# Two pads in SBUF and a new timetable for the operand sums of an expert stage on TensorE

## The chip, the core and the metric

One core of a Trainium2 chip runs the whole program in one launch. The metric is the device time of the launch in microseconds (us), taken as the median of several runs. Beside the timed runs there is one execution with a hardware profile; its rows are what the text below reads.

## The reference

Three layers follow one another on 2304 tokens of width 512, all in float32.

```python
q_s = exp(q - max_d(q)); q_s /= sum_d(q_s)
k_s = exp(k - max_s(k)); k_s /= sum_s(k_s)
x = q_s @ (k_s.T @ v)
h = x @ w_in
x = maximum(0.01 * h, h) @ w_out
logits = x @ w_gate
P = exp(logits - max(logits))
for _ in range(8):
    P /= P.sum(1); P /= P.sum(0); P *= N / E
out = sum_e P[:, e] * (maximum(x @ w1[e], 0) @ w2[e])
```

There are 4 batches of 8 heads with 576 rows of 64; the middle layer has 2048 hidden columns, and each of the 8 experts has 1024.

## The kernel before

**Operands in two parts.** TensorE reads fp32r. Nearly every float32 operand is kept as a high part and a low part, and a product takes three matmuls: high with high, high with low, low with high. One operand is stationary (128 columns, loaded by a LDWEIGHTS before each matmul) and the other moves (384 or 512 columns). The function `split` makes the two parts: ScalarE copies the operand (line 445), VectorE subtracts the copy from it (line 446).

**Stages.** The program is laid out in half steps by hand. The function `at` books a task for a half step; `half_step` first runs what is booked, then advances the running generators, then does its own piece of work. Each engine works through its instructions in the order in which they are written; in the last stage a scheduler places the instructions, and it may put some of them earlier, between those of the stage before.

1. Attention, up to about 127 us, overlapped with the start of the next stage.
2. The middle layer: 4 phases of 24 steps (6 token blocks of 384, times 4 units of 128 hidden columns). Step s has two runs of 12 matmuls of 384 columns: `first(s)` (tile `ph`: the weights `wa` or `wb` are stationary, the tokens `xs` move) and `second(s)` (tile `y`: the weights are stationary, the hidden values `hh` move). Phases 0 and 2 have their weights in `wa`, phases 1 and 3 in `wb`. After each `first`, ScalarE and VectorE make `hh` (lines 194 to 196). At the last unit of a block VectorE adds the four `y` tiles to `acc` (line 217), and the next block's `second` needs those PSUM tiles free. The last phase starts at half step 144; below, "half step +n" means 144 + n. Its blocks end at the half steps +7, +15, +23, +31, +39 and +47. From each finished block a small gate product is formed (tiles `pg` and `pt`).
3. The experts: 3 superblocks of 768 tokens, 32 groups each, 96 groups in all. The hidden layer of a group is a seven-product scheme: 7 runs of 6 matmuls of 384 columns (tiles `pa` to `pd`: parts of `wa` stationary, parts of `xs` moving). The output layer has 36 matmuls of 512 columns to a group (tile `e`: the hidden values in `xs` stationary, the weights `wb_t` moving).

**The operands of the seven products.** `x_sums(sb)` makes them for a superblock from the finished `acc` blocks: four subtractions on VectorE (line 478) and seven splits. For the first superblock it is booked at half step +31 and does one stage per half step, +31 to +38. It borrows, for the subtraction that it calls `t1`, the one buffer `s` that `pair_sums` also needs for the sums of expert weights on GpSimd.

**Where the tiles lie.** A tile begins at a multiple of 32 bytes of its partition. The pool `const` begins at byte 16,512 = 129 x 128. Ahead of `wa` it holds only tiles whose sizes sum to a multiple of 128, so that `xs` begins at 55,680 = 435 x 128 and `wa` at 135,552 = 1059 x 128. Three small tiles follow (32 bytes each), so the pool `h` with `hh` begins at 168,416 = 1315 x 128 + 96. The pools on the right side grow downwards from 229,344; `wb_t`, 32,768 bytes, begins at 196,576 = 1535 x 128 + 96. All slices that the runs of matmuls named above read begin at multiples of 512 bytes within their tiles.

Of the kernel before, what the change touches and what calls it, by code (L numbers as in the profile page):

```python
# [8 lines left out]
F32 = mybir.dt.float32  # L9
# [6 lines left out]
P = 128  # L16
# [6 lines left out]
def kernel(  # L23
# [51 lines left out]
    const = ctx.enter_context(tc.tile_pool(name="const", bufs=1))  # L75
# [23 lines left out]

    wa = const.tile([P, PU * US], F32R, name="wa")  # L100

    ml = ml_ctx.enter_context(tc.tile_pool(name="ml", bufs=2))
    att = att_ctx.enter_context(tc.tile_pool(name="att", bufs=2, side="right"))

# [300 lines left out]


    WA = {"A11": 0, "A12": 1, "S3": 2, "A22": 3, "S1": 4, "S2": 5, "S4": 6}
    XB = {"B11": 0, "T2": 1, "T1": 2, "T3": 3, "B21": 4, "B22": 5, "T4": 6}
    NQ = E * NEU // 2
    NG = NSB * NQ  # L410
    QW = KC // 2 * P
# [17 lines left out]
    def xt(name):  # L429

        j = XB[name]
        return xs[:, j * XS : (j + 1) * XS].rearrange("p (l c n) -> p l c n", l=2, c=KC // 2)
# [11 lines left out]
    def split(hi, lo, a):  # L444
        nc.scalar.copy(hi, a)  # L445
        return lambda: nc.vector.tensor_tensor(lo, a, r32(hi), op=ALU.subtract)  # L446
# [19 lines left out]
    def x_sums(sb):  # L466

        b = [
            acc[2 * sb + t].rearrange("p (k c n) -> p k c n", k=2, c=KC // 2)[:, k]
            for k in range(2)  # L470
            for t in range(2)
        ]
        b11, b12, b21, b22 = b
        pool, tag, bufs = (hp_, "hh", 2) if sb else (later["mo"], "s", 1)
        t1 = pool.tile([P, KC // 2, BLK], F32, tag=tag, name=f"t1_{sb}", bufs=bufs)

        def sub(o, x, y):
            nc.vector.tensor_tensor(o, x, y, op=ALU.subtract)

        def both(name, a):  # L480
            split(xt(name)[:, 0], xt(name)[:, 1], a)()
            ready.add(("xt", sb, name))

        def stages():
            sub(t1, b12, b11)
            sub(b12, b22, b12)
            yield 1
            both("B11", b11)
            yield
            both("B22", b22)  # L490
            yield 1
            sub(b22, b22, t1)
            both("T2", b22)
            yield
            both("T1", t1)
            yield 1
            both("T3", b12)
            yield
            both("B21", b21)
            yield 1  # L500
            sub(b21, b21, b22)
            both("T4", b21)

        for x in stages():
            if x or sb == 0:
                yield


# [131 lines left out]
    def at(t, f, *a):  # L640
        plan.setdefault(t, []).append((f, a))
# [5 lines left out]
    def half_step(t, f=None, *a):  # L647
        for g, b in plan.pop(t, ()):
            task = g(*b)
            if task is not None:  # L650
                active.append([task, None])
        now = [x for x in active if x[1] != PE_NEXT]
        then = [x for x in active if x[1] == PE_NEXT]
        advance(now)
        if f is not None:
            f(*a)
        advance(reversed(then))
        active[:] = [x for x in active if x[1] != DONE]

    def open_units():  # L660
        att_ctx.close()
        pool = ctx.enter_context(
            tc.tile_pool(name="wb", bufs=1, side="right", reuse_waits="tile")
        )
        later["wb"] = pool.tile([P, PU * US], F32R, name="wb_t")
# [40 lines left out]
    for t, (u, half) in zip((-18, -15, -12, -10, -8, -5, -2, 1), halves):  # L706
        at(t, prep_half, u, half)
    at(24, lambda: nc.sync.dma_start(wg_t, wg) and None)
    at(24, open_units)
    H2 = 2 * SP  # L710

# [6 lines left out]
    at(H2 * (NPH - 1) + 2, gate_weight)  # L718
    T3 = H2 * (NPH - 1)
    at(T3 + 8, pair0)  # L720
    at(T3 + 31, x_sums, 0)
    END = 2 * NS
    at(END + 6, balance)

# [29 lines left out]
    t = END  # L754
    for i in range(NG + 2):
        if i % NQ == NQ - 1 and i < NG - 1:
            at(t + 3, x_sums, i // NQ + 1)
        for f in group(i):
            half_step(t, f)
            t += 1  # L760
# [41 lines left out]
```

## Time and profile before

| what | value |
|---|---|
| median of 3 runs | 2042.87 us (2042.85 to 2042.97) |
| the profiled execution's own time | 2042.97 us |
| its span, first to last instruction | 2041.2 us |
| mean granted TensorE clock over the span | 0.992 of full speed |

The span is 1.8 us shorter than the execution's own time; the rest lies around it. A mean granted clock of 1 would be 2.4 GHz throughout.

### The profile page before, as it was taken

Reading aid. Unit: us, or ns where it says so; the run is one execution under the profiler, and the core shown is the slowest. Engines: PE = TensorE matmul, PEld = TensorE weight load, DVE = VectorE, ACT = ScalarE, POOL = GpSimd, SP = SyncE. Lnnn points to the kernel's source line nnn. Section 1 sums busy time; section 2 is a strip of 40 time slices with the busy share of each in tenths; the row PEclk is TensorE's granted clock in tenths of the full one; section 3 lists DMA queues with packets and bytes.
Section 4 is the critical chain, followed back from the end, with each engine's and each line's share of the span. In section 5 each row is a group of like instructions: output and inputs, shape, how many; then the busy total and the mean of one; then the engine's idle time right before and its main releaser. Section 6 shows DMA issues by size and latency. Waiting matters only on the chain.

```text
span 2041.2 us, 26341 instructions
## 1 busy us (share of the span) xinstructions
PE 2007.7 (98%) x10323; PEld 1824.1 (89%) x10323; DVE 1294.8 (63%) x1941; ACT 806.2 (39%) x1367; POOL 485.9 (24%) x476
## 2 busy tenths in 40 slices
PE   6999999999999999999999999999999999999999
PEld 5899999998889889988998899889888988898887
DVE  8746534335786666666766666666686666666663
ACT  6654323224443333333444333333344333333331
POOL 2324313200223223122132231221322312313220
PEclk8999999999999999999999999999999999999999
DMA  6502111100212212112132122121212221212210
GB/s 228 175 1 83 43 41 42 52 1 0 83 42 83 83 42 83 67 58 83 42 114 83 42 83 69 56 83 44 80 64 92 83 75 50 83 49 76 83 42 31
DMA packets 65452, 138.55 MB, mean 68 GB/s; under 512 B 4656, under 2 KB 4656, under 8 KB 65328
## 3 DMA queue, kind: packets, MB, share of 16 engines
q1 hardware_dynamic: 65328, 136.87, 19.5%
q8 instruction: 81, 1.33, 0.3%
q14 instruction: 43, 0.35, 0.1%
HBM read 132.14 MB, written 4.72 MB: 67 GB/s over the span
## 4 chain that ended last, share of the span: by engine, by line
PE 73%; DVE 1%; ACT 0%; issue 0%; DVEq 0%; ACTq 0%
PE e L178 39%; PE pc L178 10%; PE pd L178 10%; PE pa L178 10%; PE pb L178 5%; DVE wa L446 0%; PE y L178 0%; DVE xs L555 0%; ACT wa L445 0%; DVE pm L387 0%; DVE cs L388 0%; PE pt L178 0%; PE pcs L178 0%; PE pg L178 0%; DVE rs L386 0%; DVE rs L384 0%
## 5 line engine op out<-in xcount | busy, mean ns | idle before, releaser
L178 PE MATMUL e<-wb_t,xs 128*128 128x512 f32 x3456 | 822.4, 395 | 0.0
L178 PEld LDWEIGHTS e<-wb_t,xs 128*128 128x128 f32 x3456 | 647.3, 188 | 148.6
L452 POOL TENSOR_TENSOR s<-pair 128x256 f32<-128x256 f32 x96 | 73.8, 769 | 1207.2 <-DMA pair<-in_w 631.6
L548 DVE SCALAR_TENSOR_TENSOR acc<-e,pm,acc 128x512 f32<-128x512 f32 x264 | 193.2, 744 | 105.7 <-PE e L178 103.0
L178 PE MATMUL pa<-xs,wa 128*128 128x384 f32 x1152 | 231.9, 335 | 0.0
L555 DVE SCALAR_TENSOR_TENSOR xs<-c,xs 128x384 fp32r<-128x384 f32 (+1 forms) x192 | 185.8, 986 | 72.6 <-ACT xs L554 72.6
L178 PE MATMUL pc<-xs,wa 128*128 128x384 f32 x1152 | 230.8, 334 | 0.0
L178 PE MATMUL pd<-xs,wa 128*128 128x384 f32 x1152 | 230.6, 334 | 0.0
L554 ACT ACTIVATE xs<-c 128x768 fp32r<-128x768 f32 x192 | 126.7, 681 | 242.0 <-PE e L178 221.5
L178 PEld LDWEIGHTS pa<-xs,wa 128*128 128x128 f32 x1152 | 203.3, 188 | 8.5
L178 PEld LDWEIGHTS pd<-xs,wa 128*128 128x128 f32 x1152 | 202.4, 188 | 0.1
L178 PEld LDWEIGHTS pc<-xs,wa 128*128 128x128 f32 x1152 | 202.4, 188 | 0.2 <-issue 0.2
L196 DVE TENSOR_TENSOR hh<-g,hh 128x384 fp32r<-128x384 f32 x96 | 58.7, 611 | 208.3 <-ACT g L195 208.3
L446 DVE TENSOR_TENSOR wa<-s,wa 128x768 fp32r<-128x768 f32 x96 | 91.9, 957 | 101.7 <-ACT wa L445 101.6
L445 ACT CAST wa<-s 128x768 fp32r<-128x768 f32 x96 | 80.2, 835 | 168.8 <-POOL s L455 148.2
L570 DVE TENSOR_TENSOR c<-c 128x384 f32<-128x384 f32 x96 | 54.2, 564 | 134.4 <-ACT c L590 134.4
L580 ACT COPY c<-pa 128x384 f32<-128x384 f32 x96 | 46.1, 480 | 212.3 <-PE pa L178 196.9
L194 ACT ACTIVATE hh<-ph 128x384 fp32r<-128x384 f32 x96 | 47.2, 491 | 191.0 <-PE y L178 180.3
L446 DVE TENSOR_TENSOR wa<-pair,wa 128x1024 fp32r<-128x1024 f32 x96 | 120.8, 1258 | 2.6 <-ACT wa L445 2.5
L446 DVE TENSOR_TENSOR wb_t<-pair,wb_t 128x1024 fp32r<-128x1024 f32 x96 | 114.1, 1224 | 8.5 <-PE y L178 4.7
L178 PE MATMUL y<-hh,wb_t 128*128 128x384 f32 x576 | 111.8, 343 | 4.5 <-DVE acc L217 4.2
L455 POOL TENSOR_TENSOR s<-pair,s 128x256 f32<-128x256 f32 x96 | 114.2, 1190 | 7.5
(117 smaller groups left out, 2519.5 us busy)
## 6 DMA issues: line engine op xcount, KB each, us to landing
pair<-in_w SPq DMA_DIRECT2D x192, 512.0 KB, 5.0
raw<-in_wm SPq DMA_DIRECT2D x32, 512.0 KB, 3.8
v<-in_vt SPq DMA_DIRECT2D x16, 320.0 KB, 5.3
k<-in_kt SPq DMA_DIRECT2D x16, 288.0 KB, 5.5
out<-acc SPq DMA_DIRECT2D x18, 256.0 KB, 2.0
acc<-in_q SPq DMA_DIRECT2D x5, 768.0 KB, 6.1
acc<-in_q SPq DMA_DIRECT2D x3, 256.0 KB, 6.8
wg_t<-in_wg SPq DMA_DIRECT2D x1, 16.0 KB, 5.3
```

The lines of the kernel that those rows point to most:

```text
L178: nc.tensor.matmul(o, a, b, start=start, stop=stop, **more)
L194: nc.scalar.activation(hh[:, 0, :], p, AF.Prelu, alpha=0.01)
L196: nc.vector.tensor_tensor(hh[:, 1, :], g, r32(hh[:, 0, :]), op=ALU.subtract)
L445: nc.scalar.copy(hi, a)
L446: return lambda: nc.vector.tensor_tensor(lo, a, r32(hi), op=ALU.subtract)
L452: nc.gpsimd.tensor_tensor(s[:, 0], a21, a22, op=ALU.add)
L455: nc.gpsimd.tensor_tensor(s[:, 2], a12, s[:, 1], op=ALU.subtract)
L548: nc.vector.scalar_tensor_tensor(a, y, scale, a, op0=ALU.mult, op1=ALU.add)
L554: nc.scalar.activation(o[:, 0], p, AF.Relu)
L555: nc.vector.scalar_tensor_tensor(o[:, 1], p, 0.0, r32(o[:, 0]), op0=ALU.max, op1=ALU.subtract)
L570: add = lambda o, x, y: nc.vector.tensor_tensor(o, x, y, op=ALU.add)
L580: nc.scalar.copy(c1, bk[0])
```

## The change

Two pads are allocated. One of 32 bytes follows `wa` in the pool `const`: it moves the pool `h`, and all that lies after it on the left side, up by 32 bytes, so that `hh` begins at 168,448 = 1316 x 128. One of 96 bytes is the first tile on the right side: it moves `wb_t` down to 196,480 = 1535 x 128, and the attention tiles by the same 96 bytes. `xs`, `wa` and `acc` stay where they are.

The first superblock's eleven operations (four subtractions, seven splits) are booked one by one at the half steps +18 to +23, +27 to +30, and +35. Their order changes, and with it the order of the parts in `xs` (the table `XB`). For the later two superblocks `x_next` runs the same operations in five stages, as before, with the new order.

```diff
--- before.py
+++ after.py
@@ -99,6 +99,11 @@
 
     wa = const.tile([P, PU * US], F32R, name="wa")
 
+
+    const.tile([P, 8], F32, name="pad")
+    ctx.enter_context(tc.tile_pool(name="rpad", bufs=1, side="right")).tile(
+        [P, 24], F32, name="rpad"
+    )
     ml = ml_ctx.enter_context(tc.tile_pool(name="ml", bufs=2))
     att = att_ctx.enter_context(tc.tile_pool(name="att", bufs=2, side="right"))
 
@@ -405,7 +410,7 @@
 
 
     WA = {"A11": 0, "A12": 1, "S3": 2, "A22": 3, "S1": 4, "S2": 5, "S4": 6}
-    XB = {"B11": 0, "T2": 1, "T1": 2, "T3": 3, "B21": 4, "B22": 5, "T4": 6}
+    XB = {"B11": 0, "B22": 1, "T1": 2, "T3": 3, "T2": 4, "B21": 5, "T4": 6}
     NQ = E * NEU // 2
     NG = NSB * NQ
     QW = KC // 2 * P
@@ -481,28 +486,26 @@
             split(xt(name)[:, 0], xt(name)[:, 1], a)()
             ready.add(("xt", sb, name))
 
-        def stages():
-            sub(t1, b12, b11)
-            sub(b12, b22, b12)
-            yield 1
-            both("B11", b11)
-            yield
-            both("B22", b22)
-            yield 1
-            sub(b22, b22, t1)
-            both("T2", b22)
-            yield
-            both("T1", t1)
-            yield 1
-            both("T3", b12)
-            yield
-            both("B21", b21)
-            yield 1
-            sub(b21, b21, b22)
-            both("T4", b21)
-
-        for x in stages():
-            if x or sb == 0:
+        return (
+            lambda: sub(t1, b12, b11),
+            lambda: sub(b12, b22, b12),
+            lambda: both("B11", b11),
+            lambda: both("B22", b22),
+            lambda: both("T1", t1),
+            lambda: both("T3", b12),
+            lambda: sub(b22, b22, t1),
+            lambda: both("T2", b22),
+            lambda: both("B21", b21),
+            lambda: sub(b21, b21, b22),
+            lambda: both("T4", b21),
+        )
+
+    def x_next(sb):
+        f = x_sums(sb)
+        for i, n in ((0, 2), (2, 4), (4, 5), (6, 8), (5, 6), (8, 9), (9, 11)):
+            for g in f[i:n]:
+                g()
+            if n in (2, 4, 5, 8):
                 yield
 
 
@@ -657,6 +660,13 @@
         advance(reversed(then))
         active[:] = [x for x in active if x[1] != DONE]
 
+    x0 = []
+
+    def x_first(n):
+        if n == 0:
+            x0.extend(x_sums(0))
+        x0[n]()
+
     def open_units():
         att_ctx.close()
         pool = ctx.enter_context(
@@ -718,7 +728,9 @@
     at(H2 * (NPH - 1) + 2, gate_weight)
     T3 = H2 * (NPH - 1)
     at(T3 + 8, pair0)
-    at(T3 + 31, x_sums, 0)
+
+    for n, t in enumerate((18, 19, 20, 21, 22, 23, 27, 28, 29, 30, 35)):
+        at(T3 + t, x_first, n)
     END = 2 * NS
     at(END + 6, balance)
 
@@ -754,7 +766,7 @@
     t = END
     for i in range(NG + 2):
         if i % NQ == NQ - 1 and i < NG - 1:
-            at(t + 3, x_sums, i // NQ + 1)
+            at(t + 3, x_next, i // NQ + 1)
         for f in group(i):
             half_step(t, f)
             t += 1
```

## Rows read from the trace of the kernel before

**Rows 1.** The page's head: the span, and each engine's busy time (share, instructions).

```profile
span 2041.2 us, 26341 instructions
...
PE 2007.7 (98%) x10323; PEld 1824.1 (89%) x10323; DVE 1294.8 (63%) x1941; ACT 806.2 (39%) x1367; POOL 485.9 (24%) x476
```

**Rows 2.** TensorE by stretch: from:to, length, busy (instructions), granted clock, DMA.

```profile
480.00:490.00 10.00, 8.14 (x38) 0.83 0.01 2
...
600.00:2041.00 1441.00, 1437.29 (x7134) 1.00 0.20 68
```

**Rows 3.** Timeline of TensorE in the expert stage: start, us, what, matmuls.

```profile
599.69 1.20 PE L178 MATMUL pd<-xs,wa 128*128 128x384 f32 x6
600.73 8.56 PE L178 MATMUL e<-wb_t,xs 128*128 128x512 f32 x36
609.13 1.20 PE L178 MATMUL pa<-xs,wa 128*128 128x384 f32 x6
```

**Rows 4.** Matmuls of the middle layer by tile: duration min/median/max in ns.

```profile
L178 PE MATMUL ph<-xs,wa x576: 330/334/668, 55.1 to 394.5; 128*128 128x384 f32 x192
...
L178 PE MATMUL ph<-xs,wb_t x576: 335/338/522, 191.4 to 514.1; 128*128 128x384 f32 x192
...
L178 PE MATMUL y<-hh,wa x576: 333/338/632, 62.6 to 405.1; 128*128 128x384 f32 x192
...
L178 PE MATMUL y<-hh,wb_t x576: 331/334/523, 202.0 to 525.6; 128*128 128x384 f32 x192
```

**Rows 5.** Timeline of TensorE in phases 1 (wb) and 2 (wa).

```profile
206.18 2.25 PE L178 MATMUL y<-hh,wb_t 128*128 128x384 f32 x12
208.26 2.28 PE L178 MATMUL ph<-xs,wb_t 128*128 128x384 f32 x12
210.38 2.25 PE L178 MATMUL y<-hh,wb_t 128*128 128x384 f32 x12
...
308.76 2.28 PE L178 MATMUL y<-hh,wa 128*128 128x384 f32 x12
310.88 2.27 PE L178 MATMUL ph<-xs,wa 128*128 128x384 f32 x12
312.99 2.28 PE L178 MATMUL y<-hh,wa 128*128 128x384 f32 x12
```

**Rows 6.** Timeline at the block end of half step +15: [idle before <-releaser].

```profile
442.80 0.56 DVE L196 TENSOR_TENSOR hh<-g,hh 128x384 fp32r<-128x384 f32 x1 [3.65 <-ACT g L195]
443.28 1.95 DVE L217 TENSOR_TENSOR acc<-y,acc 128x384 f32<-128x384 f32 x4
...
443.98 2.32 PE L178 MATMUL y<-hh,wb_t 128*128 128x384 f32 x12
...
446.13 2.28 PE L178 MATMUL ph<-xs,wb_t 128*128 128x384 f32 x12
```

**Rows 7.** The same at half step +31.

```profile
481.47 0.84 ACT L445 CAST xs<-acc 128x768 fp32r<-128x768 f32 x1
...
482.09 0.95 DVE L478 TENSOR_TENSOR t<-acc,acc 128x768 f32<-128x768 f32 x1
...
483.95 1.95 DVE L217 TENSOR_TENSOR acc<-y,acc 128x384 f32<-128x384 f32 x4
...
484.65 3.67 PE L178 MATMUL y<-hh,wb_t 128*128 128x384 f32 x12 [1.86 <-DVE acc L217]
...
488.12 2.51 PE L178 MATMUL ph<-xs,wb_t 128*128 128x384 f32 x12
```

**Rows 8.** TensorE after the block end of half step +39.

```profile
508.50 3.63 PE L178 MATMUL y<-hh,wb_t 128*128 128x384 f32 x12 [2.35 <-DVE acc L217]
```

**Rows 9.** GpSimd before the sums of the second group's weights.

```profile
497.75 1.33 POOL L452 TENSOR_TENSOR s<-pair 128x256 f32<-128x256 f32 x1 [112.08 <-DVE xs L446]
```

**Rows 10.** Second superblock: the last split's VectorE half, and the product that reads it.

```profile
1019.80 0.95 DVE L446 TENSOR_TENSOR xs<-acc,xs 128x768 fp32r<-128x768 f32 x1
...
1023.05 1.20 PE L178 MATMUL pd<-xs,wa 128*128 128x384 f32 x6
```

## The prediction

> **What bounds the kernel now.** I read the page's head first: TensorE is busy for 2007.7 of 2041.2 us [rows 1], so only what shortens its own stream, or a gap in it, can move the end. The view by stretches separates the two: from 600 us to the end TensorE never stops (what is missing of the 1441 us is the tail), while between 480 and 490 us 1.86 us are idle and the granted clock falls to 0.83 [rows 2]. In the first place I therefore look at the spacing of matmuls, in the second at what makes TensorE wait.
>
> The spacing comes from differences of starts in the timeline, since the durations overlap. In the expert stage a run of 6 matmuls of 384 columns takes 1.04 us (599.69 to 600.73), 173.3 ns each; a run of 36 with 512 columns takes 8.40 us (600.73 to 609.13), 233.3 ns each [rows 3]. At the first one's pace per column, 512 columns would take 173.3 x 4/3 = 231.1 ns and the run 8.32 us. So `e` is 0.08 us a run slower than its width explains.
>
> The middle layer has a comparison built in. The same code runs with weights from `wa` and from `wb`, and the operand pairs differ in where they begin: `xs` and `wa` at multiples of 128 bytes, `hh` and `wb_t` 96 bytes past one. Where both of a pair begin alike the median duration is 334 ns (`ph` with `wa`, `y` with `wb`), where they differ it is 338 (`ph` with `wb`, `y` with `wa`) [rows 4]. Neither the function nor the weights' tile explains this crossing; the relative start does. By spacing, 12 matmuls of `y` with `wb` take 2.08 us, the undisturbed pace; `ph` with `wb` and `y` with `wa` 2.12; `ph` with `wa`, although alike, 2.11 [rows 5]. I read the last as a pace that settles only some matmuls after a run that was out of step. In `e`, `xs` and `wb_t` begin unlike too.
>
> **The pads.** After them `xs`, `wa`, `wb_t` and `hh` all begin at multiples of 128. They add no instruction.
>
> `e`: 96 groups x 0.08 = 7.7 us to gain if the pair settles to the pace per column. The other bounds: nothing, or the mixed pace of 384-column pairs, 0.04/12 = 3.3 ns, x 4/3 = 4.4 ns per matmul on top of today, 3456 x 4.4 = 15 us lost. I take the gain, since `e` is nearest to the products of the same stage, whose operands are already alike.
>
> Middle layer: 48 runs of each kind. `y` with `wa` and `ph` with `wb` have 48 x 0.04 = 1.9 us each, `ph` with `wa` 48 x 0.03 = 1.4. Some of the runs with `wa` lie in the loading stage up to 127 us, where other waits set the pace; I estimate a fifth, leaving 0.8 x 3.3 = 2.7. Sum 2.7 + 1.9 = 4.6 us. Bounds: 5.2 us gained, or 1.9 lost (see the third rival).
>
> The Trainium skill speaks against this part. SBUF — State Buffer, section Who interferes with whom, gives TensorE two independent read ports, one for the moving operand and one for the weight load, and says that it never waits on anyone; by that rule a relative start costs nothing and the pads bring 0. The crossing of 334 and 338 ns [rows 4] does not agree with it, if the relative start is its cause. It is a rival below.
>
> **The eleven operations.** None is added or removed for the first superblock; each subtraction is 0.95 us of VectorE, each split 0.84 of ScalarE and 0.95 of VectorE [rows 7, 10]. No DMA is issued by them. What counts is which of them stand ahead of line 217 at a block's end, for TensorE waits there: undisturbed, VectorE makes `hh` at 442.80, line 217 follows at 443.28, and the next `y` starts 0.70 us after that [rows 6].
>
> Half step +31, removed: two subtractions stand between `hh` and line 217. The next `y` starts again 0.70 us after line 217 (483.95, 484.65), having idled 1.86 us. Then it runs slowly: 3.47 us (484.65 to 488.12) [rows 7] instead of 2.15 [rows 6], 1.32 us more, in the stretch whose clock is 0.83, that is, partly at the lower of the two levels, 1.2 GHz [rows 2]. Together 3.2 us.
>
> Half step +39, removed: the last operations of the old booking, and beside them splits for the second group's weights, hold line 217 up. TensorE idles 2.35 us [rows 8]; the same slow run after it, 1.3 us, is my estimate from the one above. Together 3.65 us.
>
> Half step +23, added: the split of `T3` is booked at a block's end and is written ahead of line 217. Its copy must pass ScalarE after the two instructions that make `hh`; its subtraction then occupies VectorE for 0.95 us. So line 217 comes 0.95 to 1.3 us late and `y` with it: I take 1.2 us. This idle time is shorter than 1.86, so I count no slow clock behind it; with it, 1.3 more.
>
> The rest at +18 to +22, +27 to +30 and +35 I cost at nothing: there no block ends, and VectorE idles 3.65 us ahead of `hh` [rows 6], which covers one 0.95 us operation (without that cover each costs 0.95).
>
> Released early: GpSimd waited 112.08 us, until 497.75, for `t1`'s buffer [rows 9]. `T1` is now done at +22, so the second group's weight sums and their four split instructions can be placed earlier, from +22 on, on ScalarE and VectorE, queued ahead of `hh` and line 217. Bounds: 0, if they fall in idle time, and 0.95 + 1.3 with a slow clock if one split stands ahead of a line 217. I take 0.5.
>
> Later superblocks: the order of operations changes, the last split stays in the last stage. Today it begins at 1019.80 and its product at 1023.05 [rows 10], 2.3 us after it ends: two operations more ahead of it (1.9 us) would still be covered. Cost 0; uncovered, 2 x 1.9 us.
>
> Sum of this part: 3.2 + 3.65 - 1.2 - 0.5 = 5.15, say 5.2 us.
>
> **Sum.** 7.7 + 4.6 + 5.2 = 17.5 us. Against the profiled execution's own 2042.97 us (span 2041.2, 1.8 around it; 0.1 above the median of 2042.87): 2025.5 us.
>
> **Rivals.**
> 1. The stalls only move. The pads pay 12.3, but at +23 and at a later block end the released splits stand ahead of line 217 and cost a slow clock each, so the rebooking nets 0: 2030.7 us. For it: VectorE's queue is in order and line 217 has no slack. Against: VectorE idles most of each step.
> 2. The pads do nothing (the rule above: only a gap in the stream can be won). Then 5.2: 2037.8 us. For it: the excess of `e` could belong to its width. Against: rows 4.
> 3. 128 is not enough. `hh` begins at 0 modulo 512 after the change, `wa` and `wb_t` at 384; before, the pairs that ran alike were alike modulo 512 as well (`hh` and `wb_t`: 28,160 = 55 x 512 apart). If that is what matters, `e` and `ph` with `wb` gain 7.7 + 1.9, `y` with `wb` loses 1.9, and the `wa` runs stay: 7.7 + 5.2 = 12.9 gained, 2030.1 us.
> 4. Slower. An alike pair has been seen only with 384 columns. If 512 columns do not settle but take the mixed pace throughout, `e` loses 15 us and the rest gains 9.8: 2048.2 us. It decides from 8.40 + (9.8 + 4.1)/96 = 8.54 us per run of 36 on. Against: two of three matmuls would have to get worse than in today's unlike pair.
>
> **How the numbers follow.** 0.2% is 4.1 us, about what a measurement of this kernel can tell from no change. Forecast 0.55 (its own range 2021.5 to 2029), rival 1 0.2, rival 2 0.08, rival 3 0.12, rival 4 0.05. The low end is the forecast with 5.2 for the middle layer, 1.2 and 0.5 not lost, and 1.5 of small waits behind 520 us that go as well. The high end, 2034, takes in rivals 1 and 3 with some of their spread: 0.52 + 0.18 + 0.12 = 0.82. Faster: the forecast and rivals 1 and 3 (0.87) with 0.05 of rival 2, 0.92; same: 0.03, the rest of rival 2; slower: rival 4, 0.05.
>
> **What would show it.** Right: runs of 36 `e` at 8.32 us, all four medians of the middle layer at 334 ns, no idle TensorE at +31 and +39, one of about 1.2 us at +23 behind the split of `T3`. Wrong: `e` at 8.40 (rival 2) or above 8.54 (rival 4); `y` at 336 or more with both weights' tiles (rival 3); idle time and a clock under 1.00 at two or more block ends between 455 and 515 us (rival 1).

## The result and the profile after

The changed kernel takes 2020.03 us (median of 4 runs, 2018.37 to 2021.37) against 2042.92 us (4 runs, 2042.85 to 2043.03): a ratio of 0.9891 with a 95% interval from 0.9878 to 0.9904. It is faster, by 22.9 us where 17.5 were forecast, and the time lies 1.5 us below the low end of my range. The profiled execution took 2021.2 us with a span of 2019.4, the slower of two levels among the four runs (2018.4 and 2018.9, 2021.2 and 2021.4), for which I have no explanation.

The page's head, to be read beside [rows 1]:

```profile
PE 1989.0 (98%) x10323; PEld 1823.8 (90%) x10323; DVE 1294.2 (64%) x1941; ACT 805.7 (40%) x1367; POOL 485.6 (24%) x476
```

TensorE has the same 10323 instructions and is busy 18.7 us less. Most of the gain must therefore be in the stream itself, not in its gaps. TensorE by stretch, in the columns of [rows 2]:

```profile
480.00:500.00 20.00, 19.40 (x112) 1.00 0.00 1
...
513.00:520.00 7.00, 6.91 (x32) 0.76 0.45 150
...
600.00:2019.00 1419.00, 1415.53 (x7108) 1.00 0.20 69
```

The clock of 0.83 in the stretch of [rows 2] is gone, and 0.60 of its 1.86 us of idle time are left; but a slow stretch stands at 513. From 600 us on the stream is again unbroken: the expert stage is not less idle, it is denser. Timeline of TensorE in that stage, against [rows 3]:

```profile
595.25 8.36 PE L183 MATMUL e<-wb_t,xs 128*128 128x512 f32 x36
603.45 1.23 PE L183 MATMUL pa<-xs,wa 128*128 128x384 f32 x6
604.51 1.20 PE L183 MATMUL pb<-xs,wa 128*128 128x384 f32 x6
...
610.75 1.55 PE L183 MATMUL e<-wb_t,xs 128*128 128x512 f32 x6
```

From start to start the run of 36 `e` takes 8.20 us (595.25 to 603.45), where [rows 3] show 8.40. The first `pa` behind it takes 1.06 instead of 1.04. From one run of `e` to the next it is 15.50 us now. It was 15.68 before, by this next run's start in the timeline of before, to be subtracted from the 600.73 of [rows 3]:

```profile
616.41 1.79 PE L178 MATMUL e<-wb_t,xs 128*128 128x512 f32 x7
```

So a group gains 0.17 to 0.18 us, 0.20 at the run of `e` less 0.02 at the `pa` behind it. What the whole stage gains is read from the first and the last start of `e`, before and after:

```profile
L178 PE MATMUL e<-wb_t,xs x3456: 389/394/484, 536.8 to 2036.9; 128*128 128x512 f32 x192
L183 PE MATMUL e<-wb_t,xs x3456: 387/389/486, 531.5 to 2015.1; 128*128 128x512 f32 x192
```

From first to last it was 1500.1 us and is 1483.6, a gain of 16.5 us. That is nearly three quarters of the whole. Now the middle layer by tile, the columns of [rows 4], and then its timeline, as in [rows 5]:

```profile
L183 PE MATMUL ph<-xs,wa x576: 333/334/668, 55.0 to 393.9; 128*128 128x384 f32 x192
...
L183 PE MATMUL ph<-xs,wb_t x576: 334/334/340, 190.8 to 507.3; 128*128 128x384 f32 x192
...
L183 PE MATMUL y<-hh,wa x576: 334/337/631, 62.2 to 404.4; 128*128 128x384 f32 x192
...
L183 PE MATMUL y<-hh,wb_t x576: 331/337/522, 201.2 to 520.4; 128*128 128x384 f32 x192
```

```profile
205.44 2.28 PE L183 MATMUL y<-hh,wb_t 128*128 128x384 f32 x12
207.56 2.24 PE L183 MATMUL ph<-xs,wb_t 128*128 128x384 f32 x12
209.64 2.28 PE L183 MATMUL y<-hh,wb_t 128*128 128x384 f32 x12
...
306.19 2.25 PE L183 MATMUL ph<-xs,wa 128*128 128x384 f32 x12
308.28 2.28 PE L183 MATMUL y<-hh,wa 128*128 128x384 f32 x12
310.39 2.24 PE L183 MATMUL ph<-xs,wa 128*128 128x384 f32 x12
```

The crossing of [rows 4] has turned into a split by function: `ph` is at 334 ns with both weights' tiles, `y` at 337 with both, although `hh` begins at a multiple of 128 bytes now. `y` with `wb`, 2.08 us in [rows 5], has become slow (2.12), `ph` with `wb` has become fast (2.08).

The block ends at +23 and +31, with VectorE's part (line 217 of before is line 222 here, 446 is 451, 478 is 483):

```profile
461.54 0.56 DVE L201 TENSOR_TENSOR hh<-g,hh 128x384 fp32r<-128x384 f32 x1 [1.56 <-ACT g L200]
...
462.26 0.96 DVE L451 TENSOR_TENSOR xs<-acc,xs 128x768 fp32r<-128x768 f32 x1 [0.16 <-ACT xs L450]
463.13 1.48 DVE L222 TENSOR_TENSOR acc<-y,acc 128x384 f32<-128x384 f32 x3
463.83 0.94 PE L183 MATMUL y<-hh,wb_t 128*128 128x384 f32 x4 [1.15 <-DVE acc L222]
...
480.91 0.94 DVE L451 TENSOR_TENSOR wa<-s,wa 128x768 fp32r<-128x768 f32 x1
481.78 0.94 DVE L483 TENSOR_TENSOR acc<-acc,acc 128x768 f32<-128x768 f32 x1
482.65 0.54 DVE L201 TENSOR_TENSOR hh<-g,hh 128x384 fp32r<-128x384 f32 x1
483.12 1.47 DVE L222 TENSOR_TENSOR acc<-y,acc 128x384 f32<-128x384 f32 x3
483.80 0.93 PE L183 MATMUL y<-hh,wb_t 128*128 128x384 f32 x4 [0.60 <-DVE acc L222]
...
503.19 1.12 PE L183 MATMUL y<-hh,wb_t 128*128 128x384 f32 x5
...
512.42 0.27 PE L183 MATMUL pt<-wa 16*128 16x8 f32 x1 [1.30 <-ACT wa L358]
```

At +23 the split of `T3` (462.26) stands between `hh` and line 222, and TensorE idles 1.15 us. At +31 it idles 0.60 instead of the 1.86 of [rows 7]: a released split of `wa` (480.91) and the subtraction booked at +30 (481.78) hold up `hh` itself, and line 222 follows at once. At +39 (503.19) the idle time of [rows 8] is gone. The 1.30 us at 512.42 wait for ScalarE's copy of the gate product `pg` (line 358, 353 before). They stand in the trace of before too, at 519.26, where the clock stays at 1.00; here the clock of 513 to 520 is 0.76, partly at 1.2 GHz, and from this `pt` to the next `pb` it takes 8.13 us (512.42 to 520.55) instead of 6.55 (519.26 to 525.81).

### The profile page after: what moved, and what is told of

Same layout as the page of the kernel before. It is cut to its first block, busy times and chain, and to the rows that moved or that the text cites. A ratio compares the mean times of both kernels' runs of the same rounds, so it can differ in the third digit from the quotient of the medians.

```text
span 2019.4 us, 26343 instructions
## 1 busy us (share of the span) xinstructions
PE 1989.0 (98%) x10323; PEld 1823.8 (90%) x10323; DVE 1294.2 (64%) x1941; ACT 805.7 (40%) x1367; POOL 485.6 (24%) x476
## 4 chain that ended last, share of the span: by engine, by line
PE 73%; DVE 1%; ACT 0%; issue 0%; ACTq 0%; DVEq 0%
PE e L183 38%; PE pa L183 10%; PE pc L183 10%; PE pd L183 10%; PE pb L183 5%; PE y L183 0%; DVE wa L451 0%; DVE xs L558 0%; ACT wa L450 0%; DVE pm L392 0%; DVE cs L393 0%; PE pcs L183 0%; PE pt L183 0%; PE pg L183 0%; DVE rs L391 0%; DVE rs L389 0%
## 5 line engine op out<-in xcount | busy, mean ns | idle before, releaser
L183 PE MATMUL e<-wb_t,xs 128*128 128x512 f32 x3456 | 803.4, 390 | 0.0
L183 PE MATMUL pb<-xs,wa 128*128 128x384 f32 x576 | 115.3, 334 | 0.0
```

The source lines that it names most:

```text
L183: nc.tensor.matmul(o, a, b, start=start, stop=stop, **more)
```

## The experiments

Each ratio is against runs of the kernel before on the same chip (medians 2041.7 us, 15 runs, for the first four; 2043.2, 9 runs, for the others). Where operands begin decides most of them, so here are the starts of the four tiles, in bytes modulo 512, worked out from the tiles' sizes:

| kernel | `xs` | `wa` | `hh` | `wb_t` |
|---|---|---|---|---|
| before, e2 | 384 | 384 | 480 | 480 |
| after, e1 | 384 | 384 | 0 | 384 |
| e3, e6, e7 | 384 | 384 | 384 | 384 |
| e4 | 480 | 480 | 480 | 480 |
| e5 | 384 | 384 | 0 | 256 |
| e8 | 384 | 384 | 0 | 320 |

**e1, the pads alone**, in the kernel before:

```
+    const.tile([P, 8], F32, name="pad")
+    ctx.enter_context(tc.tile_pool(name="rpad", bufs=1, side="right")).tile(
+        [P, 24], F32, name="rpad"
+    )
```

> The two pads alone, with the operand sums booked as in the kernel before. Theory (settled pace): nearly all of the gain is in the expert stage, where a 512-column matmul whose two operands begin alike settles at 512/2.4 + 13.3 = 226.7 ns instead of 231.1 or more. Runs of 36 e take 8.20 us as in the changed kernel, the group 15.50, which is 96 x 0.18 = 17.3 us; the middle layer adds about 1. Time 2024 to 2025.5 us, and the stalls at half steps +31 and +39 stay (about 2 us idle each). Rival (booking): the pads bring no more than the 8.32 us run that was predicted, 7.7 us, and the rest comes from the new booking. Time 2031 us or more.

Measured 2025.0 us, ratio 0.9918 (0.9904 to 0.9932). `e` falls as in the kernel after, to a median of 389 ns, and the stalls at +31 and +39 are still there:

```profile
482.83 3.47 PE L182 MATMUL y<-hh,wb_t 128*128 128x384 f32 x12 [1.89 <-DVE acc L221]
...
506.51 3.31 PE L182 MATMUL y<-hh,wb_t 128*128 128x384 f32 x12 [2.43 <-DVE acc L221]
...
909.12 8.36 PE L182 MATMUL e<-wb_t,xs 128*128 128x512 f32 x36
917.33 1.23 PE L182 MATMUL pa<-xs,wa 128*128 128x384 f32 x6
```

**e2, the booking alone**: the kernel after without these four lines.

> The new booking alone, without the pads. Theory (settled pace): only the stalls at the block ends change, 4 to 6 us. Time 2037 to 2039 us; runs of 36 e stay at 8.40 us. Rival (booking): more than 8 us, 2035 us or less, if what the stage gained in the changed kernel came from when its operands and weights are ready.

Measured 2036.79 us, 0.9976 (0.9967 to 0.9985): 4.9 us of 2041.7. `e` stays at 8.40 us a run (910.11 to 918.51). The two parts add up, 0.82% and 0.24% against 1.09% together.

```profile
910.11 8.56 PE L179 MATMUL e<-wb_t,xs 128*128 128x512 f32 x36
918.51 1.20 PE L179 MATMUL pa<-xs,wa 128*128 128x384 f32 x6
```

**e3, all four alike modulo 512**: the kernel after with a larger pad, which moves `hh`.

```
-    const.tile([P, 8], F32, name="pad")
+    const.tile([P, 104], F32, name="pad")
```

> The changed kernel with a pad of 416 bytes in place of 32, so that hh begins at 384 modulo 512 like xs, wa and wb_t. Theory (settled pace, modulo 512 or 256): y settles too. Median y duration 334 ns with both weights' tiles, runs of 12 in 2.08 us where they took 2.115; 96 runs x 0.035 = 3.4 us less than the changed kernel, about 2016.7 us. Rival (a multiple of 128 is all that counts, and y is slow since its moving operand is freshly written or for its place in the step): y stays at 337 ns, 2020 us.

The median is 334 ns for `y` with both tiles, and 12 matmuls of any kind take 2.08 us. Timed, it is 2017.76 us, 0.9882 (0.9869 to 0.9896), an interval that overlaps with that of after, so the time alone wouldn't show it. The tiles do:

```profile
L183 PE MATMUL y<-hh,wa x576: 334/334/630, 60.2 to 400.3; 128*128 128x384 f32 x192
...
L183 PE MATMUL y<-hh,wb_t x576: 333/334/688, 198.8 to 517.3; 128*128 128x384 f32 x192
...
L183 PE MATMUL ph<-xs,wa x576: 334/334/668, 53.2 to 389.9; 128*128 128x384 f32 x192
...
L183 PE MATMUL ph<-xs,wb_t x576: 334/334/338, 188.4 to 502.5; 128*128 128x384 f32 x192
```

From the first `ph` with `wb` to the last with `wa`, which is phases 1 and 2, it takes 201.5 us (188.4 to 389.9), where the kernel after takes 203.1 (190.8 to 393.9): 1.6 us for half of the phases, and 24 x (0.04 + 0.03) = 1.7 are expected. The span of the profiled run, 2016.3 us, is 3.1 below that of after; that this is near the 3.4 expected for all four phases is partly luck, since the slow stretch is longer here (clocks of 0.75 from 506 to 513 us and 0.77 to 520).

**e4, alike, but none at a multiple of 128**: a pad ahead of `acc` and a larger one behind `wa`, none on the right.

```
+    const.tile([P, 24], F32, name="pad0")
     ...
-    const.tile([P, 8], F32, name="pad")
-    ctx.enter_context(tc.tile_pool(name="rpad", bufs=1, side="right")).tile(
-        [P, 24], F32, name="rpad"
-    )
+    const.tile([P, 104], F32, name="pad")
```

> As the run before, but xs, wa, wb_t and hh all begin 96 bytes past a multiple of 128, alike modulo 512 (480). No operand begins at a multiple of 128. Theory (only the relative start counts): the same as with hh alike at multiples of 128: e in runs of 8.20 us, all medians 334 ns, about 2016.7 us. Rival (the start itself must be a multiple of 128 bytes, as the change is named): e back at 8.40 us a run or slower, 2034 us or more.

Measured 2017.71 us, 0.9879 (0.9864 to 0.9895): as fast as e3, with all of its medians, though every operand begins 96 bytes past a multiple of 128. The multiple isn't needed; being alike is enough.

```profile
L181 PE MATMUL e<-wb_t,xs x3456: 387/389/478, 529.4 to 2013.0; 128*128 128x512 f32 x192
```

**e5, all at multiples of 128, `wb_t` 128 bytes lower**: the kernel after with

```
-        [P, 24], F32, name="rpad"
+        [P, 56], F32, name="rpad"
```

> The changed kernel with wb_t 128 bytes lower: still all operands at multiples of 128, but xs against wb_t (e, ph with wb) now 128 bytes apart modulo 512, y with wb 256 apart, y with wa 128 apart as in the changed kernel. Theory (only a pair alike modulo 512 settles): e does not settle, its runs of 36 are back near 8.40 us, ph with wb at 337 ns or more like y; time 2037 to 2041 us. Rival (a multiple of 128 is enough, y is slow for another reason): e at 8.20 us and 2020 us. Between the two: y with wb at 334 ns would say that 256 is enough.

Measured 2037.09 us, 0.9970 (0.9958 to 0.9981): what the pads give to `e` is lost, 916.32 - 907.92 = 8.40 us a run, as before the change. So multiples of 128 aren't enough either. `y` with `wb` settles at 334 ns although its operands begin 256 bytes apart modulo 512, `ph` with `wb`, 128 apart, does not (337):

```profile
907.92 8.56 PE L183 MATMUL e<-wb_t,xs 128*128 128x512 f32 x36
916.32 1.21 PE L183 MATMUL pa<-xs,wa 128*128 128x384 f32 x6
```

```profile
L183 PE MATMUL ph<-xs,wb_t x576: 334/337/343, 191.2 to 507.5; 128*128 128x384 f32 x192
...
L183 PE MATMUL y<-hh,wb_t x576: 332/334/445, 201.8 to 519.1; 128*128 128x384 f32 x192
```

**e8, `wb_t` 64 bytes lower**: the same edit with `[P, 40]`.

> The changed kernel with wb_t 64 bytes lower: xs against wb_t 64 bytes apart (e, ph with wb), y with wb 192 apart. Theory (modulo 512): nothing of these settles; e near 8.40 us a run of 36, ph with wb and y above 336 ns; 2037 to 2041 us. Rival (what matters is smaller than 64 bytes): e at 8.20 us, 2020 us.

Measured 2035.22 us, 0.9960 (0.9945 to 0.9975), below the 2037 to 2041 that were expected. `e` is slow (913.86 - 905.47 = 8.39 us a run), but `ph` with `wb`, 64 bytes apart, takes 2.08 us for 12 at a median of 336 ns: for 384 columns this distance costs nothing from start to start, for 512 it does. `y` with `wb`, 192 apart, lies between, at 2.09 to 2.10 us and 336 ns. That nothing would settle was wrong for `ph`.

```profile
202.04 2.24 PE L183 MATMUL ph<-xs,wb_t 128*128 128x384 f32 x12
204.12 2.26 PE L183 MATMUL y<-hh,wb_t 128*128 128x384 f32 x12
...
905.47 8.56 PE L183 MATMUL e<-wb_t,xs 128*128 128x512 f32 x36
913.86 1.21 PE L183 MATMUL pa<-xs,wa 128*128 128x384 f32 x6
```

**e6, `e` in halves of 256 columns**, in e3, to see how the settled time goes with the width:

```
+        for v in (slice(0, DM // 2), slice(DM // 2, DM)):
             for j in range(2):
                 ...
-                    mm(y, hh, w2(i)[:, 0, u], beg, False)
+                    mm(y[:, v], hh, w2(i)[:, 0, u, v], beg, False)
```

(and so for the other two products.)

> The kernel with hh alike modulo 512, with each e matmul of 512 columns made as two of 256 (72 in place of 36 to a group; the sums are the same). Theory (a settled matmul costs its columns at 2.4 GHz and a fixed 13.3 ns): 256/2.4 + 13.3 = 120.0 ns, a run of 72 takes 8.64 us where 36 took 8.20, 96 x 0.44 = 42 us more, about 2060 us. Rival (a price per column, 13/12 of a cycle, as the prediction took it): 115.6 ns, 8.32 us a run, 2029 us. A third way, 2070 us or more, would say that the weight load of 128 columns becomes the bound at this width.

A run of 72 takes 919.84 - 911.21 = 8.63 us, 119.9 ns a matmul; the pace per column would make 8.32. The kernel is slower, 2057.69 us, 1.0070 (1.0054 to 1.0087).

```profile
911.21 8.79 PE L183 MATMUL e<-wb_t,xs 128*128 128x256 f32 x72
919.84 1.21 PE L183 MATMUL pa<-xs,wa 128*128 128x384 f32 x6
```

**e7, no booking at a block end**, in e3:

```
-    for n, t in enumerate((18, 19, 20, 21, 22, 23, 27, 28, 29, 30, 35)):
+    for n, t in enumerate((18, 19, 20, 21, 22, 24, 27, 28, 29, 32, 35)):
```

> The kernel with hh alike modulo 512, with the split of T3 booked at half step +24 in place of +23 and the last subtraction at +32 in place of +30, so that neither stands ahead of line 217 at a block's end. Theory (line 217 has no slack): the idle time of about 1.1 us at +23 and of about 0.6 at +31 go, 2016.1 us where the other booking gave 2017.8. Rival (the stall only moves to another block end): no change, 2017.8 us.

Measured 2015.0 us, 0.9861 (0.9846 to 0.9876), the fastest here. Its interval lies just below that of the kernel after, but it overlaps with that of e3, from which it differs by two bookings alone; the trace has to decide. The `y` runs behind +23, +31 and +39 begin without an idle gap. The 1.30 us ahead of `pt` remain, and the clock behind them is 1.00 in this execution:

```profile
458.61 2.32 PE L183 MATMUL y<-hh,wb_t 128*128 128x384 f32 x12
...
477.88 2.32 PE L183 MATMUL y<-hh,wb_t 128*128 128x384 f32 x12
...
506.32 0.27 PE L183 MATMUL pt<-wa 16*128 16x8 f32 x1 [1.30 <-ACT wa L358]
...
508.68 4.46 PE L183 MATMUL y<-hh,wb_t 128*128 128x384 f32 x24
```

```profile
513.00:520.00 7.00, 7.00 (x42) 1.00 0.00 0
```

In e3 the same 24 `y` stand in the slow stretch:

```profile
510.61 7.04 PE L183 MATMUL y<-hh,wb_t 128*128 128x384 f32 x24
```

The span of e7 is 4.5 us below that of e3 (2016.3 to 2011.8). The two gaps of e3, 1.15 and 0.67 us, are 1.8 of it, and they moved to no other block end. The 24 `y` behind `pt`, 7.04 us in e3 and 4.46 here, are 2.6. That the new booking brought the full clock isn't shown: e5 and e8, booked as the kernel after, have it too (1.00 from 506 to 520 us).

## Why the prediction was wrong where it was

**The failed step is the size of `e`.** "At the first one's pace per column, 512 columns would take 173.3 x 4/3 = 231.1 ns": this took the whole 173.3 ns to grow with the width. Settled pairs show 119.9 ns at 256 columns (e6), 173.3 at 384 [rows 3], and 226.7 at 512: the run of 36 in the kernel after, 8.20 us, is some 9 matmuls of 224 to 236 ns and then 27 of 226.7. Both steps of 128 columns add 53.4 ns, 0.417 ns a column, which is one cycle of 2.4 GHz, and 13.3 ns are left over at every width. So 512 columns take 213.3 + 13.3 = 226.7 ns, and today's 233.3 were 6.6 ns, not 2.2 ns, above a settled pace. The term was 7.7 us and measures 16.5; that excess of 8.8 us is more than the 5.4 between forecast and result, and the middle layer, which brought nothing of its 4.6, hid a part of it. With one settled width in view, the price of another had two readings, in proportion or with a fixed part, and I took the first without the second as a bound.

**The mechanism of the pads was right**, though not what it took as alike: e1 and e2 put 0.82% on the pads and 0.24% on the booking, and the relative start decides. Rival 2 falls with that. It was drawn from the Trainium skill (SBUF — State Buffer, Who interferes with whom), which gives TensorE two independent read ports and says that it never waits on anyone. That placement is free, as rival 2 read it, does not agree with e5 against the kernel after: 8.40 and 8.20 us a run with nothing but 128 bytes between them.

**In the middle layer rival 3 was right, the forecast wrong.** `y` stays slow with both tiles because `hh` begins at 0 where `wa` and `wb_t` begin at 384 modulo 512, and in e3, where `hh` begins at 384 as well, it settles. By spacing, an undisturbed run of 12 takes 0.04 us more for `y` with `wb`, and 0.04 less for `ph` with `wb`, 0.01 less for `y` with `wa` and 0.02 less for `ph` with `wa`; that would be 0.03 x 48 = 1.4 us instead of 4.6. Even this does not arrive: phases 1 and 2 take 203.1 us before (191.4 to 394.5, [rows 4]) and 203.1 after (190.8 to 393.9), since those runs aren't all: the longer ones of `ph` at the block ends went from about 2.35 us up to 2.38 to 2.40. There the middle layer gained nothing, as rival 3 had it. `ph` with `wa`, whose own operands begin alike throughout, takes 2.11 us beside the `y` of before, 2.09 beside that of after and 2.08 in e3, so the run beside it counts too, as the prediction read it. The modulus of rival 3 was too strict: in e5 a pair 256 bytes apart settles, at 384 columns (a pair of 512 columns wasn't tried at that distance). For `e`, rival 3 had the same pace per column and fell short with the forecast. Rival 4, the slower one, needed runs above 8.54 us; they take 8.20.

**The booking** was forecast at 5.2 us and measures 4.9 by itself (e2). That the sums are so near is partly luck, since the slow stretch behind 513 us stands in no term and costs 1.6 us in the profiled execution of the kernel after (8.13 - 6.55), 1.8 in that of e2; whether it falls into every run, and what was then gained where no term stands, isn't shown. Point by point: idle time at +39 gone, as forecast; 1.15 us at +23 behind the split of `T3`, forecast 1.2, without a slow clock, as forecast; 0.60 us at +31, forecast 0 there with 0.5 for released splits at some block end. That is rival 1 in small: the released work does stand ahead of a line 222, with the subtraction of +30, but the stall is a third of the old one. The later superblocks cost nothing, as forecast: from 600 us on no gap is left ahead of the tail. One reason in that step was wrong: GpSimd waited for the last reader of `t1`, the subtraction at +27, and not for the split of `T1` at +22. It starts at 474.82, released by line 483:

```profile
474.82 0.74 POOL L457 TENSOR_TENSOR s<-pair 128x256 f32<-128x256 f32 x1 [89.26 <-DVE acc L483]
```

**The sum** of what was measured, 16.5 + 0 + 4.9 = 21.4 us, stands against 22.9 between the medians and 21.8 between the two profiled executions. The rest is of the size by which runs of one kernel differ here. The pads alone agree with it: 16.7 us in e1 (2041.7 to 2025.0).

**Open**: why a pair settles at one relative start and not at another (that the load of the next weights and the stream of the moving operand get in each other's way is only argued), why some 9 matmuls pass before `e` settles, and what decides whether a slow stretch follows the 1.30 us ahead of `pt`.

## What to carry to other kernels

Where a long stream of matmuls has no gaps, compare the spacing of the same shape with different operands: a difference of 1 to 3% that goes with where stationary and moving operand begin relative to each other is won by a pad of some tens of bytes. Being alike modulo 512 bytes was enough here for every pair with no unlike run beside it, modulo 256 for the one pair of 384 columns that tried it, while a multiple of 128 was neither needed nor sufficient. Before scaling a matmul's time to another width, find its fixed part from two widths; with one width alone, carry both readings into the range. And book spare work in the steps between block ends, since an operation that fits into the idle time of one step makes a stall in another.

## What was not expected of the hardware

A settled matmul with its weight load costs its columns at one a cycle and 13.3 ns on top at 256, 384 and 512 columns alike, so halving the width of `e` made the kernel 0.7% slower than before (e6). Operands 96 bytes apart cost 3.3 ns a matmul at 384 columns and 6.6 at 512 [rows 3, 5], and 64 bytes of distance cost nothing between starts at 384 but nearly the full price at 512 (e8, 8.39 us a run). An idle time of 1.30 us at the same instruction, the first `pt` of the block that ends at +39, was followed by a slow stretch in five of the ten profiled executions (after, e2, e3, e4, e6; a clock of 0.76 in the kernel after) and by a full clock in the other five (before, e1, e5, e7, e8). In the kernel after one of 1.15 us was followed by a full clock, in the kernel before one of 1.86 by a slow one.
